# An attention and two-layer MoE kernel: v's block rows in the key buffers, key windows by DMA, and w_out's words loaded ahead of their conversion

## Chip, cores and metric

The kernel runs on one core of a Trainium2 chip. The metric is device time in microseconds (us) of one execution; three runs of a kernel are shown by their median. A profile is one more execution, with its own time.

## What is computed

Three stages follow one another. Attention works per head on 768 tokens with a window of 16 to either side, and on 24 block summaries (the maximum of the keys and the mean of the values over 32 tokens). The result goes through two feed-forward layers; the first has a softmax gate and a layer norm.

```python
k_sum = k.reshape(B, H, nb, block, D).max(axis=3)
v_sum = v.reshape(B, H, nb, block, D).mean(axis=3)
scores_all = np.concatenate([scores_l_m, scores_s], axis=-1)   # near keys (masked), block keys
a = softmax(scores_all);  attn = a @ np.concatenate([v, v_sum], axis=2)
...
h = x @ w_in;  solu = h * softmax(h)
ln = (solu - mu) / np.sqrt(var + 1e-06) * g_ln
x = ln @ w_out
...
h = x @ w_in2;  out = elu(h) @ w_out2
```

Weights come as float64, q, k and v as float32; B, H, S, D are 2, 8, 768, 64, the model width is 512, the layers 1024 and 2048 wide, and there are 1536 tokens.

## The kernel before

Attention is cut into 24 units of 64 queries, 12 for each of the two batches. Unit n has four steps: `attn_s(n)` copies the unit's 96 keys from `k_sb` into a window buffer `kw` on GpSimd (POOL), makes the scores on TensorE (PE, tile `s_ps`), adds the mask on VectorE (DVE, `sm`), takes the exponential on ScalarE (ACT) and divides on POOL; `attn_p(n)` transposes (`p_ps`, copied to `pT`); `attn_x(n)` multiplies with the value window `vw` (`x_ps`) and splits the result into a high and a low part `xT`. Every product of the two layers is three matmuls of such halves (`mm3x`). The first layer takes 128 tokens (j) at a time: products in `h`, a row maximum and two passes over 1024 columns for the norm (`ffn1_ln`), transposes to `t_ps` that ACT copies and DVE splits into `lnT` (`ffn1_tr`), and products with `w_out` in `y_ps`.

`convert` makes a float32 pair out of float64 words: a DMA of the words into a slot, an absolute value on ACT (`conv`), a clamp on POOL, three integer operations on DVE, and a copy on ACT and a difference on DVE for the two halves. The slots lie in the tiles `y0` to `y2` (shown as y_65 to y_67), two in each, which hold the first layer's result only later; the six are `early`. w_in's eight chunks use the slots in turn, w_out's eight chunks use two slots (`early[k % 2]`), and for w_out the layer norm's gain `gT` is multiplied in on POOL. The mean of v's blocks (`sum_v`, matmuls to `vs_ps`) reads six row tiles `v_rows`, which lie in y1 and y2, so in the same memory as four of the six slots.

A loop over 24 ticks sets the order of the calls. Tick t makes half of a row of the first layer (`mm_in`), the scores of unit t+6, the transposes of unit t+4 and the values of unit t+3; a dictionary `converts` says in which ticks w_out's chunks are converted. For SyncE (SP), which issues all DMAs, this order is kept as it is written. On the other engines a scheduler orders the instructions at build time, and each engine then runs them in that order. The four PSUM buffers of the tag "b" are shared by `vs_ps`, `s_ps`, `p_ps`, `x_ps`, `t_ps` and `y_ps`. A DMA gets one of eight semaphores in turn, so that a DMA is issued only when the one eight places ahead has landed.

Of the kernel before, what the change touches and what calls it, by code (L numbers as in the profile page):

```python
# [49 lines left out]
def tile_kernel(ctx: ExitStack, tc: tile.TileContext, qd, kT, v, w_in, w_out, g_ln, w_in2, w_out2,  # L50
                ident_d, mask_d, avg_d, out):
    nc = tc.nc
    scale = 1.0 / math.sqrt(D)
# [7 lines left out]

    y = [com.tile([128, KD, TC], F32, name=f"y{i}") for i in range(NTOK // TC)]
    flat = [t.rearrange("p d s -> p (d s)") for t in y]
    rows = [[t[:, i * DM:(i + 1) * DM] for i in range(KD * TC // DM)] for t in flat]
    stage = [[t.bitcast(I32)[:, i * 1024:(i + 1) * 1024].rearrange("p (k f) -> p k f", k=KD)
              for i in range(KD * TC // 1024)] for t in flat]

# [3 lines left out]
    p_k = ctx.enter_context(tc.tile_pool(name="p_k", bufs=1, side="left", reuse_waits="tile"))  # L71
    p_at = tc.alloc_tile_pool(name="p_at", bufs=2, side="left", reuse_waits="tile")
# [6 lines left out]
    w_out_hl = [chunk(p_w, "w", KF1, "w_out") for _ in range(KF1)]  # L79
    lnT_hl = [p_w.tile([128, KF1, TB], F32R, tag=f"lnT{i}", name="lnT") for i in range(2)]  # L80
    gT = p_ln.tile([128, KF1], F32, name="gT")
    negh = p_ln.tile([128, 1], F32, name="negh")
    dump = p_ln.tile([128, F1], BF16, name="dump")
    mask = p_at.tile([128, 3, KW], F32, name="mask", bufs=1)
    kws = [p_at.tile([128, NP, KW], F32, name=f"kw{i}", bufs=1) for i in range(NBUF)]
    vws = [p_at.tile([128, DM], F32, name=f"vw{i}", bufs=1) for i in range(NBUF)]
    avg = p_at.tile([128, 128 + NB], F32, name="avg", bufs=1)
    nc.gpsimd.memset(negh, -0.5)

    def copy_pool(out_, in_):  # L90
        nc.gpsimd.tensor_scalar(out_, in_, 1.0, 0.0, op0=ALU.mult, op1=ALU.add)


    def lo_of(out_, x, hi):
        nc.vector.tensor_tensor(out_, x, hi.bitcast(F32), op=ALU.subtract)  # L95
# [7 lines left out]

    def convert(bits, src, hi, lo, g=None):
        nc.sync.dma_start(bits, src if len(src.shape) == 3 else src.rearrange("p (k f) -> p k f", k=KD))
        words = bits.rearrange("p k (f two) -> p k f two", two=2)
        low, high = words[:, :, :, 0], words[:, :, :, 1]
        hi, lo = (t if len(t.shape) == 3 else t.rearrange("p (k f) -> p k f", k=KD) for t in (hi, lo))  # L110
        a = p_k.tile([128, KD, 128], I32, tag="conv", name="conv", bufs=3)
        x = a.bitcast(F32)
        nc.scalar.activation(x, high.bitcast(F32), AF.Abs)  # L113
        nc.gpsimd.tensor_scalar(x, x, F64_HUGE, F64_TINY, op0=ALU.min, op1=ALU.max)  # L114
        nc.vector.tensor_scalar(a, a, 3, 0x3FFFFFF8, op0=ALU.logical_shift_left, op1=ALU.bitwise_and)
        nc.vector.scalar_tensor_tensor(a, high, -0x40000000, a, op0=ALU.bitwise_and, op1=ALU.bitwise_or)
        nc.vector.scalar_tensor_tensor(a, low, 29, a, op0=ALU.logical_shift_right, op1=ALU.bitwise_or)
        if g is not None:
            nc.gpsimd.tensor_scalar(x, x, g, 0.0, op0=ALU.mult, op1=ALU.add)
        nc.scalar.activation(hi, x, AF.Copy)  # L120
        lo_of(lo, x, hi)

    early = stage[0] + stage[1] + stage[2]
    v_rows = rows[1] + rows[2]

    def load_w_in(n, k):
        cs = slice(n * 512, (n + 1) * 512)
# [1 line left out]
                w_in_hl[0][:, k, cs], w_in_hl[1][:, k, cs])  # L129

    def load_w_out(k):
        convert(early[k % 2], w_out[k * 128:(k + 1) * 128, :].bitcast(I32), *w_out_hl[k], gT[:, k:k + 1])


    k_sb, q_bd, xT, live, ksum, vsum = {}, {}, {}, {}, {}, {}
# [13 lines left out]

    def sum_v(b):  # L150
        pst = psb.tile([128, DM], F32, tag="b", name="vs_ps")
        for i in range(S // 128):
            vt = v_rows[i]
            nc.sync.dma_start(vt, v[b, PAD + i * 128:PAD + (i + 1) * 128, :])
            c0 = NB - i * 4
            nc.tensor.matmul(pst, lhsT=avg[:, c0:c0 + 128], rhs=vt, start=i == 0, stop=i == S // 128 - 1)
        vsum[b] = p_at.tile([128, DM], F32, tag="vsum", name="vsum", bufs=1)
        nc.scalar.activation(vsum[b][WIN:KW, :], pst[WIN:KW, :], AF.Copy)

    def load_q(n):  # L160
        q_bd[n] = p_at.tile([128, NP, 2 * TQ], F32, tag="q", name="q_bd", bufs=4)
        nc.sync.dma_start(q_bd[n], qd[n])

    def load_v(n):
        b, t = divmod(n, NT)
        nc.sync.dma_start(vws[n % NBUF][0:WIN, :], v[b, t * TQ:t * TQ + WIN, :])

    def attn_s(n):
        b, t = divmod(n, NT)
        j, half = divmod(n, 2)  # L170
        kw = kws[n % NBUF]
        if n not in q_bd:
            load_q(n)
        if t < NBUF and n:
            copy_pool(kw[:, :, WIN:KW], ksum[b])
        copy_pool(kw[:, :, 0:WIN], k_sb[b][:, :, t * TQ:t * TQ + WIN])
        sps = psb.tile([128, NP, 128], F32, tag="b", name="s_ps")
        for p in range(NP):
            nc.tensor.matmul(sps[:, p, 0:KW], lhsT=q_bd[n][:, p, :], rhs=kw[:, p, :], start=True, stop=True)  # L179
        sm = p_at.tile([128, NP, KW], F32, tag="sm", name="sm", bufs=NBUF)  # L180
        st = p_at.tile([128, 4, NP], F32, tag="st", name="st", bufs=NBUF)
        nm, ss, ri = (st[:, i, :] for i in range(3))
        mi = 1 if t == 0 else (2 if t == NT - 1 else 0)
        for p in range(NP):
            nc.vector.tensor_tensor_reduce(sm[:, p, :], sps[:, p, 0:KW], mask[:, mi, :], -scale, 3.0e38,
                                           op0=ALU.add, op1=ALU.min, accum_out=nm[:, p:p + 1])
        for p in range(NP):
            nc.scalar.activation(sm[:, p, :], sm[:, p, :], AF.Exp, bias=nm[:, p:p + 1], scale=-1.0,
                                 accum_out=ss[:, p:p + 1])
        nc.vector.tensor_scalar(ri, ss, 1e-9, None, op0=ALU.add)  # L190
        nc.vector.reciprocal(ri, ri)  # L191
        for p in range(NP):
            nc.gpsimd.tensor_scalar(sm[:, p, :], sm[:, p, :], ri[:, p:p + 1], 1.0, op0=ALU.mult, op1=ALU.mult)  # L193
        live[n] = sm
# [132 lines left out]


    conv = [lambda n=n, k=k: load_w_in(n, k) for n in range(2) for k in range(KD)]
    conv += [lambda k=k: load_w_out(k) for k in range(KF1)]  # L330

    def more(n=1):
        for _ in range(n):
            if conv:
                conv.pop(0)()
# [57 lines left out]
    for i, t in ((0, 11), (1, 17)):  # L393
        for d in range(KD):
            after[t + d].append((mm_out, i, d))
    converts = {3: 2, 4: 1, 6: 1, 9: 2, 10: 2}
    NU = B * NT
    for t, (j, n) in enumerate(ticks):
        s_n, p_n, x_n = t + LEAD, t + LEAD - 2, t + LEAD - 3
        if t == 0:  # L400
            sum_v(1)
        elif t == 1:
            load_k(1)
        elif t == 3:
            sum_k(1)
        if x_n < NU and t:
            load_v(x_n)
        if s_n < NU:
            for u in (s_n + 1, s_n):
                if u < NU and u not in q_bd:  # L410
                    load_q(u)
            attn_s(s_n)
        mm_in(j, n)
        if p_n < NU:
            attn_p(p_n)
        for f, *args in after[t]:
            f(*args)
        if x_n < NU:
            attn_x(x_n)
        more(converts.get(t, 0))  # L420
        if t in (13, 15, 17, 18, 19, 20, 21, 22):
            load_w3()
        if x_n == NU - 1:
            p_at.release()
            p_w3 = ctx.enter_context(tc.tile_pool(name="p_w3", bufs=1, side="left", reuse_waits="tile"))
            lnT_last = [p_w3.tile([128, KF1, TB], F32R, tag=f"lnT{c}", name="lnT") for c in range(2)]
# [35 lines left out]
             f == 0, f == KF2 - 1)  # L462

    def store(i, ops, t):
        o = rows[0][t]
        r0 = i * TC + t * 128
        if i == NTOK // TC - 1 and t == NTT - 1:
            for c in range(2):
                cs = slice(c * 256, (c + 1) * 256)
                if c:  # L470
                    nc.vector.tensor_copy(o[:, cs], ops[t][:, cs])
                else:
                    nc.scalar.activation(o[:, cs], ops[t][:, cs], AF.Copy)
# [84 lines left out]
```

## Time and profile before

| | us |
|---|---|
| median of 3 runs (lowest to highest) | 510.34 (509.59 to 511.14) |
| the profiled execution, its own time | 507.9 |
| span of the profile | 505.8 |
| TensorE busy | 483.2 |
| VectorE, ScalarE, GpSimd busy | 283.5, 261.8, 131.0 |
| mean granted TensorE clock, as a share of 2.4 GHz | 0.993 |

Busy time is the time in which an engine ran at least one instruction. What the profiled execution's own time has over its span lies before and after the program's instructions.

### The profile page before, as it was taken

To read this page: it belongs to the slowest core of one execution; us is meant where nothing else is said; L and a number is where in the kernel's file an instruction comes from. 1 tells how busy PE (TensorE), PEld (TensorE's weight loads), DVE (VectorE), ACT (ScalarE), POOL (GpSimd) and SP (SyncE) were. 2 spreads that over 40 slices of the span, in tenths; PEclk is the share of its full clock that TensorE was granted. 3 is DMA by queue.
4 is the path that set the end of the run, shared out by engine and by line. 5 is a ranking of instruction groups with operands and counts; after the bars stand their busy time and mean duration, and the time that the engine had idled before them with its cause. 6 is when DMAs were issued, how large, how long until landed. Compare 5 with 4: busy or idle time off the path is not lost.

```text
span 505.8 us, 7269 instructions
## 1 busy us (share of the span) xinstructions
PE 483.2 (96%) x2616; PEld 400.5 (79%) x2616; DVE 283.5 (56%) x680; ACT 261.8 (52%) x592; POOL 131.0 (26%) x216
## 2 busy tenths in 40 slices
PE   1789997999999999999999999999999999999997
PEld 1466876888988888999888888888888888888885
DVE  3689799798458747797999622351222235122222
ACT  1675896776568436655767433352323335232333
POOL 1867688688413321322232100000000000000000
PEclk9999998999999999999999999999999999999999
DMA  8989473171313400565454000020000002000002
GB/s 302 286 296 311 132 231 120 38 233 39 115 59 116 141 1 0 208 172 166 155 173 126 1 0 0 1 84 1 1 1 0 0 1 84 1 0 0 1 0 83
DMA packets 24563, 46.53 MB, mean 92 GB/s; under 512 B 2256, under 2 KB 11088, under 8 KB 24528
## 3 DMA queue, kind: packets, MB, share of 16 engines
q1 hardware_dynamic: 24528, 46.08, 28.6%
q8 instruction: 20, 0.33, 0.3%
q14 instruction: 15, 0.12, 0.1%
HBM read 42.93 MB, written 3.15 MB: 91 GB/s over the span
## 4 chain that ended last, share of the span: by engine, by line
PE 88%; DMA 3%; DVE 3%; ACT 2%; POOL 1%; issue 1%; SPq 1%; ACTq 0%; POOLq 0%
PE h L98 13%; PE h L100 13%; PE h L99 13%; PE o_ps L98 9%; PE o_ps L99 9%; PE o_ps L100 9%; PE y_ps L98 5%; PE y_ps L100 4%; PE s_ps L179 4%; PE y_ps L99 4%; PE x_ps L215 2%; DMA q_bd<-in_qd 2%; PE p_ps L198 2%; PE t_ps L254 1%; DMA k_sb<-in_kT 1%
## 5 line engine op out<-in xcount | busy, mean ns | idle before, releaser
L454 DVE SCALAR_TENSOR_TENSOR m<-m,h 128x512 f32<-128x512 f32 x48 | 32.9, 685 | 120.0 <-ACT m L453 119.8
L452 ACT ACTIVATE m<-h 128x512 f32<-128x512 f32 x48 | 28.7, 598 | 107.5 <-PE h L100 107.2
L99 PE MATMUL h<-y_hl,w 128*128 128x512 f32 x192 | 75.9, 395 | 0.0
L100 PE MATMUL h<-y_hl,w 128*128 128x512 f32 x192 | 75.9, 395 | 0.0
L98 PE MATMUL o_ps<-w,g_hl 128*128 128x512 f32 x192 | 75.5, 393 | 0.0
L99 PE MATMUL o_ps<-w,g_hl 128*128 128x512 f32 x192 | 75.4, 393 | 0.0
L98 PE MATMUL h<-y_hl,w 128*128 128x512 f32 x192 | 75.2, 395 | 0.0
L100 PE MATMUL o_ps<-w,g_hl 128*128 128x512 f32 x192 | 66.9, 392 | 0.0
L114 POOL TENSOR_SCALAR conv<-conv 128x512 f32<-128x512 f32 x48 | 36.4, 761 | 67.2 <-ACT conv L113 65.9
L193 POOL TENSOR_SCALAR sm<-sm,st 128x120 f32<-128x120 f32 x96 | 44.9, 484 | 16.7 <-DVE st L191 15.8
L95 DVE TENSOR_TENSOR g_hl<-m,g_hl 128x512 fp32r<-128x512 f32 x48 | 33.9, 707 | 24.4 <-ACT g_hl L455 24.4
L455 ACT ACTIVATE g_hl<-m 128x512 fp32r<-128x512 f32 x48 | 30.3, 630 | 32.5 <-DVE m L454 32.5
L179 PE MATMUL s_ps<-kw,q_bd 128*128 128x120 f32 x192 | 29.6, 301 | 15.9 <-DMA q_bd<-in_qd 13.3
L98 PE MATMUL y_ps<-lnT,w_out 128*128 128x384 f32 x128 | 44.0, 344 | 0.3 <-DVE lnT L95 0.2
L100 PE MATMUL y_ps<-lnT,w_out 128*128 128x384 f32 x128 | 43.1, 338 | 0.0
L99 PE MATMUL y_ps<-lnT,w_out 128*128 128x384 f32 x128 | 43.1, 336 | 0.0
L99 PEld LDWEIGHTS h<-y_hl,w 128*128 128x128 f32 x192 | 36.1, 188 | 8.6
L98 PEld LDWEIGHTS o_ps<-w,g_hl 128*128 128x128 f32 x192 | 36.1, 188 | 8.5
L100 PEld LDWEIGHTS h<-y_hl,w 128*128 128x128 f32 x192 | 36.1, 188 | 8.5
L98 PEld LDWEIGHTS h<-y_hl,w 128*128 128x128 f32 x192 | 36.1, 188 | 8.5
L100 PEld LDWEIGHTS o_ps<-w,g_hl 128*128 128x128 f32 x192 | 36.1, 188 | 8.2
L99 PEld LDWEIGHTS o_ps<-w,g_hl 128*128 128x128 f32 x192 | 36.1, 188 | 8.2
(77 smaller groups left out, 913.1 us busy)
## 6 DMA issues: line engine op xcount, KB each, us to landing
y<-in_w_in SPq DMA_DIRECT2D x20, 512.0 KB, 4.6
y<-in_w_out SPq DMA_DIRECT2D x16, 512.0 KB, 4.3
q_bd<-in_qd SPq DMA_DIRECT2D x24, 256.0 KB, 5.0
vw<-in_v SPq DMA_DIRECT2D x24, 192.0 KB, 4.2
bits<-in_w_out SPq DMA_DIRECT2D x8, 512.0 KB, 3.5
k_sb<-in_kT SPq DMA_DIRECT2D x8, 400.0 KB, 5.5
y<-in_v SPq DMA_DIRECT2D x12, 256.0 KB, 5.4
out<-y SPq DMA_DIRECT2D x11, 256.0 KB, 2.3
```

The lines of the kernel that those rows point to most:

```text
L95: nc.vector.tensor_tensor(out_, x, hi.bitcast(F32), op=ALU.subtract)
L98: nc.tensor.matmul(ps, lhsT=l[0][ls], rhs=r[0][rs], start=first, stop=False)
L99: nc.tensor.matmul(ps, lhsT=l[0][ls], rhs=r[1][rs], start=False, stop=False)
L100: nc.tensor.matmul(ps, lhsT=l[1][ls], rhs=r[0][rs], start=False, stop=last)
L114: nc.gpsimd.tensor_scalar(x, x, F64_HUGE, F64_TINY, op0=ALU.min, op1=ALU.max)
L179: nc.tensor.matmul(sps[:, p, 0:KW], lhsT=q_bd[n][:, p, :], rhs=kw[:, p, :], start=True, stop=True)
L193: nc.gpsimd.tensor_scalar(sm[:, p, :], sm[:, p, :], ri[:, p:p + 1], 1.0, op0=ALU.mult, op1=ALU.mult)
L198: nc.tensor.transpose(pps[:KW, p, :], live[n][:, p, :], ident)
L215: nc.tensor.matmul(xps[ds, p, :], lhsT=vw[:KW, p * 128 + hh * D:p * 128 + (hh + 1) * D], rhs=pT[:KW, p, hh * TQ:(hh + 1) * TQ], start=True ...
L452: nc.scalar.activation(m, h2, AF.Relu, scale=-1.0)
L454: nc.vector.scalar_tensor_tensor(m, m, -1.0, h2, op0=ALU.add, op1=ALU.max)
L455: nc.scalar.activation(gh, m, AF.Copy)
```

## The change

1. `sum_v` loads v's rows into a tile `v_sb` of the pool that holds `k_sb` (tag "k", two buffers) and no longer into y1 and y2. The two buffers serve k of batch 0, v of batch 0, v of batch 1 and k of batch 1, the last three one after the other in the same memory.
2. There are four `kw` buffers in place of three. From unit 12 on (batch 1) a DMA fills the key window (`load_kw`), one tick ahead; POOL copies it for units 0 to 11 only.
3. w_out's words go into all six slots (`early[k % 6]`), and their DMAs stand apart from the conversions: `fetches` issues them in ticks 2 to 9, `converts` makes the conversions in ticks 4 to 10. The first ACT instruction of each such conversion keeps its place in the order of the calls (`pin`).
4. The gain is multiplied in by ACT's copy (`scale=g`) and by DVE's difference; POOL's multiplication is gone.
5. One of the second layer's early conversions (`load_w3` in tick 17 or 18) moves behind the ticks: there are seven in place of eight, in other ticks.

```diff
-    rows = [[t[:, i * DM:(i + 1) * DM] for i in range(KD * TC // DM)] for t in flat]
+    rows = [t[:, i * DM:(i + 1) * DM] for t in flat[:1] for i in range(KD)]
...
+    def load_words(bits, src):
         nc.sync.dma_start(bits, src if len(src.shape) == 3 else src.rearrange("p (k f) -> p k f", k=KD))
...
-        nc.scalar.activation(x, high.bitcast(F32), AF.Abs)
+        first = nc.scalar.activation(x, high.bitcast(F32), AF.Abs)
+        if pin:
+            tc.keep_in_program_order(first)
...
-        if g is not None:
-            nc.gpsimd.tensor_scalar(x, x, g, 0.0, op0=ALU.mult, op1=ALU.add)
-        nc.scalar.activation(hi, x, AF.Copy)
-        lo_of(lo, x, hi)
+        if g is None:
+            nc.scalar.activation(hi, x, AF.Copy)
+            lo_of(lo, x, hi)
+        else:
+            nc.scalar.activation(hi, x, AF.Copy, scale=g)
+            nc.vector.scalar_tensor_tensor(lo, x, g, hi.bitcast(F32), op0=ALU.mult, op1=ALU.subtract)
...
     def load_w_out(k):
-        convert(early[k % 2], w_out[k * 128:(k + 1) * 128, :].bitcast(I32), *w_out_hl[k], gT[:, k:k + 1])
+        load_words(early[k % 6], w_out[k * 128:(k + 1) * 128, :].bitcast(I32))
+
+    def convert_w_out(k):
+        convert(early[k % 6], None, *w_out_hl[k], gT[:, k:k + 1], pin=True)
...
+        v_sb = p_k.tile([128, NP, S + 2 * PAD], F32, tag="k", name="v_sb", bufs=2).rearrange("p a s -> p (a s)")
         for i in range(S // 128):
-            vt = v_rows[i]
+            vt = v_sb[:, i * DM:(i + 1) * DM]
...
+    def load_kw(n):
+        b, t = divmod(n, NT)
+        if NCOPY <= n < B * NT:
+            nc.sync.dma_start(kws[n % NKW][:, :, 0:WIN],
+                              kT[b, :, :, t * TQ:t * TQ + WIN].rearrange("p d s -> d p s"))
...
-        copy_pool(kw[:, :, 0:WIN], k_sb[b][:, :, t * TQ:t * TQ + WIN])
+        if n < NCOPY:
+            copy_pool(kw[:, :, 0:WIN], k_sb[b][:, :, t * TQ:t * TQ + WIN])
...
-    converts = {3: 2, 4: 1, 6: 1, 9: 2, 10: 2}
+    converts = {4: 1, 5: 1, 6: 1, 7: 1, 8: 1, 9: 1, 10: 2}
+    fetches = {2: 1, 3: 1, 4: 1, 5: 1, 6: 1, 7: 1, 8: 1, 9: 1}
...
+            load_kw(s_n + 1)
             attn_s(s_n)
...
-        more(converts.get(t, 0))
-        if t in (13, 15, 17, 18, 19, 20, 21, 22):
+        for _ in range(fetches.get(t, 0)):
+            words.pop(0)()
+        for _ in range(converts.get(t, 0)):
+            parts.pop(0)()
+        if t in (13, 15, 19, 20, 21, 22, 23):
             load_w3()
```

The order of the instructions shows at three places. The first is SP near the start, where v's rows of batch 0 are loaded and behind them two chunks of w_in's words and the queries of unit 2 (`q_bd`); first before:

```order
L154 DMA y_66<-in_v 128x512 x4
L154 DMA y_67<-in_v 128x512 x2
L107 DMA y_66<-in_w_in 128x1024 x2
L162 DMA q_bd<-in_qd 128x512
L166 DMA vw_103<-in_v 96x512
L374 DMA gT<-in_g_ln 128x8
```

The same place with the change:

```order
L168 DMA v_sb<-in_v 128x512 x6
L109 DMA y_66<-in_w_in 128x1024 x2
L176 DMA q_bd<-in_qd 128x512
L180 DMA vw_104<-in_v 96x512
L396 DMA gT<-in_g_ln 128x8
```

Nothing changes its place there, but the two chunks of words no longer go into memory that v's rows occupy.

The second place is PE in tick 6, where the first rows of the first layer are transposed (`t_ps`); before, between the products of one row and the scores of unit 13:

```order
L100 MATMUL h<-w_in_83,xT 128x512
L198 MATMUL p_ps<-ident,sm 120x128
L254 MATMUL t_ps<-ident,ln 128x128 x2
L198 MATMUL p_ps<-ident,sm 120x128
L254 MATMUL t_ps<-ident,ln 128x128
L198 MATMUL p_ps<-ident,sm 120x128 x2
L254 MATMUL t_ps<-ident,ln 128x128 x13
L215 MATMUL x_ps<-pT,vw_102 64x64 x8
L179 MATMUL s_ps<-kw_100,q_bd 128x120 x4
```

The same place with the change, from the last four transposes on (ahead of them stand the unit's `p_ps` x4, `t_ps` x4, three products, `t_ps` x8 and nine products):

```order
L101 MATMUL h<-w_in_84,xT 128x512
L102 MATMUL h<-w_in_83,xT 128x512
L275 MATMUL t_ps<-ident,ln 128x128 x4
L236 MATMUL x_ps<-pT,vw_103 64x64 x8
L200 MATMUL s_ps<-kw_100,q_bd 128x120 x4
```

Sixteen transposes in one piece have become pieces of 4, 8 and 4, with 3 and 9 products of `h` between them.

The third place is DVE at the same point of the program, where the low halves of `lnT` are made; before:

```order
L234 TENSOR_REDUCE st<-h 128x1
L115 TENSOR_SCALAR conv<-conv 128x512
L95 TENSOR_TENSOR lnT<-t_ps,lnT 128x4x128
L116 SCALAR_TENSOR_TENSOR conv<-y_65,conv 128x512
L237 SCALAR_TENSOR_TENSOR ln,st<-h,ln 128x1024
L239 TENSOR_SCALAR st<-st 128x1
L117 SCALAR_TENSOR_TENSOR conv<-y_65,conv 128x512
L95 TENSOR_TENSOR lnT<-t_ps,lnT 128x4x128
```

The same place with the change:

```order
L125 SCALAR_TENSOR_TENSOR conv<-y_65,conv 128x512
L262 SCALAR_TENSOR_TENSOR st<-st 128x1
L126 SCALAR_TENSOR_TENSOR conv<-y_65,conv 128x512
L97 TENSOR_TENSOR lnT<-t_ps,lnT 128x4x128 x3
L264 SCALAR_TENSOR_TENSOR st<-st 128x1
L255 TENSOR_REDUCE st<-h 128x1
```

A conversion's two operations and a pass over a row of `h` stood between the first and the second `lnT`; now three stand together, and the row maximum comes behind them. From the program's start to the second `lnT`, DVE has two L115, two L116, two L117, one difference for w_out, one L234 and one L237 fewer than before (counted in the whole order).

## Rows read from the trace of the kernel before

**Rows 1.** Page, part 1: busy time of each engine.
```profile
PE 483.2 (96%) x2616; PEld 400.5 (79%) x2616; DVE 283.5 (56%) x680; ACT 261.8 (52%) x592; POOL 131.0 (26%) x216
```

**Rows 2.** Waits of PE: line, what it waited for, us in total, times, longest.
```profile
PE s_ps L179 <- DMA q_bd<-in_qd: 13.3, 2, 10.9
```

**Rows 3.** Stretches: length, busy us (PE, PEld, DVE, ACT, POOL), clock, DMA, GB/s.
```profile
10.00:15.00 5.00, 4.11 (x18) 3.67 (x19) 1.52 (x15) 2.40 (x10) 1.63 (x3) 1.00 1.04 393
15.00:20.00 5.00, 5.00 (x16) 2.28 (x14) 4.80 (x15) 2.59 (x10) 4.38 (x7) 1.00 0.79 238
...
25.00:30.00 5.00, 4.79 (x49) 3.89 (x47) 2.81 (x20) 3.09 (x14) 1.83 (x4) 0.74 1.03 380
60.00:85.00 25.00, 22.29 (x172) 18.07 (x171) 23.97 (x82) 21.57 (x64) 19.65 (x35) 1.00 0.46 134
85.00:100.00 15.00, 14.88 (x119) 12.44 (x119) 11.23 (x38) 10.03 (x32) 9.29 (x15) 0.89 0.30 103
100.00:120.00 20.00, 20.00 (x138) 16.99 (x135) 18.31 (x63) 15.31 (x45) 16.36 (x28) 1.00 0.52 158
300.00:350.00 50.00, 50.00 (x218) 40.49 (x217) 15.71 (x22) 19.31 (x31) 0.00 (x0) 1.00 0.06 22
```

**Rows 4.** Chain that ended last, 14 to 30 us: start, us, what.
```profile
14.36 3.69 PE vs_ps L156 x8
...
18.43 5.69 DMA q_bd<-in_qd
...
24.26 2.03 PE s_ps L179 x8
...
27.97 1.10 PE s_ps L179 x8
```

**Rows 5.** Timeline of SP: start, us, DMAs issued.
```profile
8.91 3.47 SPq L154 DMA_DIRECT2D y<-in_v  x6
16.35 2.04 SPq L107 DMA_DIRECT2D y<-in_w_in  x2
```

**Rows 6.** Timeline of POOL, 22 to 25 us.
```profile
22.63 2.56 POOL L91 TENSOR_SCALAR vw<-vsum 24x512 f32<-24x512 f32 x3
```

**Rows 7.** Timeline of PE, 20 to 22 and 81 to 87 us; in brackets the idle time ahead.
```profile
20.47 1.34 PE L198 MATMUL p_ps<-ident,sm 128*120 128x128 f32 x4 [0.28 <-POOL sm L193]
...
81.77 0.69 PE L215 MATMUL x_ps<-pT,vw 120*64 120x64 f32 x16 [0.29 <-DVE lnT L95]
84.87 1.43 PE L179 MATMUL s_ps<-kw,q_bd 128*128 128x120 f32 x8 [2.42 <-DVE lnT L95]
```

**Rows 8.** Timeline of DVE, 79 to 86 us.
```profile
79.14 1.23 DVE L234 TENSOR_REDUCE st<-h 128x1 f32<-128x1024 f32 x1 [0.65 <-PE h L100]
80.28 0.42 DVE L115 TENSOR_SCALAR conv<-conv 128x512 int32<-128x512 int32 x1
...
81.63 0.68 DVE L116 SCALAR_TENSOR_TENSOR conv<-y,conv 128x512 int32<-128x512 int32 x1
82.23 1.22 DVE L237 SCALAR_TENSOR_TENSOR ln<-h,ln 128x1024 f32<-128x1024 f32 x1
...
83.44 0.78 DVE L117 SCALAR_TENSOR_TENSOR conv<-y,conv 128x512 int32<-128x512 int32 x1
84.14 0.68 DVE L95 TENSOR_TENSOR lnT<-t_ps,lnT 128x512 fp32r<-128x512 f32 x1
84.74 0.87 DVE L95 TENSOR_TENSOR w_out<-conv,w_out 128x512 fp32r<-128x512 f32 x1
```

**Rows 9.** Groups of instructions: line, operation, count | busy us, mean ns | idle ahead.
```profile
L91 POOL TENSOR_SCALAR kw<-k_sb 128x384 f32<-128x384 f32 x24 | 13.7, 573 | 20.8 <-PE s_ps L179 12.9 <-DMA k_sb<-in_kT 7.1 <-PE p_ps L198 0.5
L119 POOL TENSOR_SCALAR conv<-conv,gT 128x512 f32<-128x512 f32 x8 | 5.5, 693 | 2.0 <-DVE conv L117 2.0
L116 DVE SCALAR_TENSOR_TENSOR conv<-y,conv 128x512 int32<-128x512 int32 x36 | 26.7, 742 | 0.3
```

**Rows 10.** DMAs issued in 12.0 to 12.4 us: count, KB each, us to landing.
```profile
y<-in_v SPq DMA_DIRECT2D x1, 256.0 KB, 5.5
```

More of the change, by code (lines that the diff above doesn't have):

```diff
@@ L37 @@
 NBUF = 3
+NKW = 4
+NCOPY = 12
 NG = 6
@@ L84, in tile_kernel @@
     mask = p_at.tile([128, 3, KW], F32, name="mask", bufs=1)
-    kws = [p_at.tile([128, NP, KW], F32, name=f"kw{i}", bufs=1) for i in range(NBUF)]
+    kws = [p_at.tile([128, NP, KW], F32, name=f"kw{i}", bufs=1) for i in range(NKW)]
     vws = [p_at.tile([128, DM], F32, name=f"vw{i}", bufs=1) for i in range(NBUF)]
@@ L100, in mm3x, with convert @@
         nc.tensor.matmul(ps, lhsT=l[1][ls], rhs=r[0][rs], start=False, stop=last)
-    def convert(bits, src, hi, lo, g=None):
+    def load_words(bits, src):
         nc.sync.dma_start(bits, src if len(src.shape) == 3 else src.rearrange("p (k f) -> p k f", k=KD))
+    def convert(bits, src, hi, lo, g=None, pin=False):
+        if src is not None:
+            load_words(bits, src)
         words = bits.rearrange("p k (f two) -> p k f two", two=2)
@@ L117, in convert @@
         nc.vector.scalar_tensor_tensor(a, low, 29, a, op0=ALU.logical_shift_right, op1=ALU.bitwise_or)
-        if g is not None:
-            nc.gpsimd.tensor_scalar(x, x, g, 0.0, op0=ALU.mult, op1=ALU.add)
-        nc.scalar.activation(hi, x, AF.Copy)
-        lo_of(lo, x, hi)
+        if g is None:
[4 more added lines that the diff above has]
+            nc.vector.scalar_tensor_tensor(lo, x, g, hi.bitcast(F32), op0=ALU.mult, op1=ALU.subtract)
     early = stage[0] + stage[1] + stage[2]
-    v_rows = rows[1] + rows[2]
     def load_w_in(n, k):
@@ L170, in attn_s @@
         j, half = divmod(n, 2)
-        kw = kws[n % NBUF]
+        kw = kws[n % NKW]
         if n not in q_bd:
             load_q(n)
-        if t < NBUF and n:
+        if t < NKW and n:
             copy_pool(kw[:, :, WIN:KW], ksum[b])
-        copy_pool(kw[:, :, 0:WIN], k_sb[b][:, :, t * TQ:t * TQ + WIN])
+        if n < NCOPY:
+            copy_pool(kw[:, :, 0:WIN], k_sb[b][:, :, t * TQ:t * TQ + WIN])
         sps = psb.tile([128, NP, 128], F32, tag="b", name="s_ps")
@@ L329, in tile_kernel @@
     conv = [lambda n=n, k=k: load_w_in(n, k) for n in range(2) for k in range(KD)]
-    conv += [lambda k=k: load_w_out(k) for k in range(KF1)]
+    words = [lambda k=k: load_w_out(k) for k in range(KF1)]
+    parts = [lambda k=k: convert_w_out(k) for k in range(KF1)]
     def more(n=1):
@@ L464, in store @@
     def store(i, ops, t):
-        o = rows[0][t]
+        o = rows[t]
         r0 = i * TC + t * 128
```

## The prediction

> **What bounds the kernel now.** I read the busy times first: PE is busy in 483.2 of 505.8 us, no other engine in more than 56% [rows 1]. Only PE's 22.6 idle us, and time in which it runs slower than it could, are there to be won. In the second layer there is none: from 300 to 350 us PE is busy in all of 50.00 at full clock, DVE in 15.71 [rows 3], and the change leaves that code alone. So I looked at PE's waits and then at the chain around each.
>
> The largest is the start: the first scores wait 10.9 us for queries, and 2 such waits make 13.3 [rows 2]. The loads ahead of that first wait are the same before and after the change. The other wait for queries, 13.3 - 10.9 = 2.4 us, ends at 24.26, and the chain tells its cause: PE multiplies v's rows from 14.36 to 18.05, this releases an issue on SP, the queries of unit 2 are issued at 18.43, land 5.69 us later, and PE starts [rows 4]. SP had last issued before that with v's rows, 8.91 to 12.38, and came to the next words of w_in only at 16.35 [rows 5]: these words go into memory that v's rows occupied. While SP stood, the DMA engines ran dry: 393 GB/s in 10 to 15 us, 238 in 15 to 20 [rows 3].
>
> The last large hole lies at 81 to 85 us: after 16 transposes the values of unit 9 wait 0.29 and the scores of unit 13 wait 2.42 us for a subtraction on DVE that frees a PSUM buffer [rows 7]. DVE was not idle then. In its row stood a conversion's operations and a pass over a row of h: 81.63, 82.23, 83.44, and only at 84.14 the subtraction [rows 8]. From 60 to 85 us DVE is busy in 23.97 of 25.00 [rows 3]; there it sets the pace.
>
> Both holes cost a second time. The granted clock is 0.74 in 25 to 30 us, and 0.89 in 85 to 100, which at two levels (1.2 and 2.4 GHz) is 15 x 0.11 = 1.65 us of lost work [rows 3]; in each case PE had just stood for more than 2.3 us.
>
> **The start.** v's rows now have memory of their own, so w_in's two chunks wait only for the DMA eight places ahead to land, and SP goes on where it stopped, at 12.38. From there on what counts is the bytes under way: the last of v's rows is issued at about 12.05 (the last 0.33 of the piece that ends at 12.38) and lands 5.5 us later, at 17.5 [rows 5, 10]; behind them 2 x 524 KB at 393 GB/s take 2.67 us and the queries' 262 KB 0.67, so these land at 20.8, in place of 18.43 + 5.69 = 24.1. PE ends its transposes at 20.47 + 1.34 = 21.8 [rows 7] and goes on at once. The scores take 1.1 us at full clock [rows 4], to 22.9. Then comes a new wait: the values of units 0 and 1 need POOL's copies of the block means, three from 22.63 to 25.19, so 0.85 each [rows 6]; the first is done at 23.5, the second at 24.3. With 0.6 us for each unit's values (81.77: 0.69 in which the last overlaps the next [rows 7]) the scores of unit 3 start at 25.0, against 27.97. Gain 2.97, taken as **3.0 us**. Bounds: without POOL's wait 24.3, a gain of 3.7; if the clock still falls through the shorter waits, about 1.3 less (24.26: 2.03 against 1.10, and the values a third longer), 1.7.
>
> Whether it lasts depends on DVE, full from 60 to 85 us: the gain reaches that stretch only if DVE's work, which w_in's words feed, moves forward as well. The words land earlier by as much as the queries do, so I let it last.
>
> **The hole at 81.** Transposes now come as 4, 8 and 4 with 3 and 9 products between, and three subtractions stand together on DVE. Nine products alone give PE 9 x 0.23 = 2.1 us in which the buffers come free. Ahead of the second subtraction DVE has less to do: two L115 (0.42), two L116 (0.68), two L117 (0.78), one L95 (0.87), one L234 (1.23) and one L237 (1.22) fewer, together 7.1 us [rows 8]. So DVE should be early there by more than the 2.71 us that PE waited. I leave 0.3 us as a wait and take **2.4 us**, and the clock's 1.65, **1.7 us**. Bounds: 0 and 2.7 for the wait, 0 and 1.7 for the clock.
>
> **Given back on DVE.** The 7.1 us are moved, not gone: all eight conversions must be done before the first y_ps is complete. From 85 to 100 us DVE idles 15.00 - 11.23 = 3.77 us, from 100 to 120 another 1.69 [rows 3]. These take 5.5; the rest, 7.1 - 5.5 = 1.6, delays y_ps: **-1.6 us**. Bounds: 0, if the products that the new order puts between y_ps cover it, and -7.1 if the idle time can't be used.
>
> **Costed at nothing.** POOL's multiplications (8 x 0.69) and 12 of its 24 copies (0.57 each) go [rows 9]; POOL was not what ended a wait of PE there, except for units 2 and 3. DVE's difference keeps its size, 128x512. The 12 new DMAs of 197 KB each (262 KB land in 5.5 us even in a full queue [rows 10]) stand right behind the queries of the same unit, and after 24.26 no scores waited for queries [rows 2]; DMA share is 0.46, 0.30 and 0.52 there [rows 3]. If that cover went, each lateness would count once per unit. w_out's words no longer hold up SP's queue until a conversion is done. The conversion that moves behind the ticks costs DVE about 2.7 us between 210 and 300; PE's first need of its product comes seven tiles later, so nothing.
>
> **POOL's share of DVE's time.** L116 reads two SBUF operands and takes 0.742 us on average [rows 9], 0.68 at 81.63 [rows 8]; over the 36 this is 2.2 us if POOL is the cause. Of POOL's work some 12.4 of the page's 131.0 us go, so between 0 and 2.2; I put 0 into the sum and half, 1.1, into its upper bound. The Trainium skill (SBUF — State Buffer, section "Who interferes with whom") says that DVE with two SBUF inputs and a GpSimd operation that reads SBUF exclude each other for the whole instruction. By it the 12.4 us of POOL work that go could free as much of DVE; the trace agrees with it in direction, with 0.742 against 0.68 us.
>
> **Sum.** 3.0 + 2.4 + 1.7 - 1.6 = 5.5 us, on the profiled execution 507.9 - 5.5 = 502.4. Its 507.9 is 2.4 under the median of the runs, 510.34, so the median becomes **504.8**. The forecast's own range is from 3.7 + 2.7 + 1.7 + 0 + 1.1 = 9.2 (501.1) to 3.6 us of gain (506.7).
>
> **Rivals.**
> - *One hole only* (gain 1.5 to 3.6, at 3.0: 507.3). The hole at 81 stays in another form: four PSUM buffers are shared by 16 transposes, values and scores as before, and DVE still has a row maximum and a conversion behind the third subtraction. For it: DVE is 96% busy there. Against it: the 7.1 us.
> - *DVE takes it all* (within 0.3%, at 510). k of batch 1 must now wait until v's products of batch 1 are done on PE, and DVE's maxima of those keys stand in its row. If they come 3 us late, the start's gain is gone, and with the -7.1 bound so is the second. Against it: the new order puts these maxima behind the last conversion of w_in.
> - *Slower: late key windows.* From unit 12 on the scores need a DMA in rows of 384 bytes. It decides if 12 windows come late by more than 5.5 / 12 = 0.46 us each; at 0.9 us each the time is 504.8 + 10.8 = 515.6. For it: each is behind queries and values in one queue. Against it: DMA share and the missing waits named above.
>   Twice the 0.5 us that 197 KB take at 393 GB/s [rows 3] would add 0.5 us per window, if nothing hid it: 12 x 0.5 = 6.0, so 510.8.
>   The Trainium skill (DMA: Bandwidth & Descriptors, section "Specifications") asks for 512 bytes and more for line rate and names a read-modify-write below; no row here shows it.
>
> **Chances.** Forecast 0.56; more than its range 0.06; one hole only 0.16; within 0.3% 0.12; slower 0.10. A run of this kernel can't tell less than 0.3% (1.5 us) from no change. Faster is 0.56 + 0.06 + 0.16 = 0.78. The range 501.1 to 509.3 leaves out the slower case, the upper half of the unchanged one and a tail below: 0.10 + 0.06 + 0.03.
>
> **What would show it.** Right: the scores of unit 2 start near 21.8 us with no wait for queries, unit 3's near 25.0; no wait over 1 us of PE for lnT around 76 to 82; clock 1.00 in both stretches; DVE over 90% busy from 85 to 115. Wrong: PE waits for kw DMAs after 70 us, for y_ps's w_out, or the DVE maxima of k idle for their DMA at 43 to 47.

## The result, and the profile after

The change makes the kernel faster: median 502.58 us of four runs (502.39 to 502.74) against 510.4 of four runs of before (509.59 to 511.14), ratio 0.984, 95% interval 0.983 to 0.986. The profiled executions are 5.5 us apart (507.9 and 502.39), just the forecast sum. The medians are 7.8 apart, 2.3 more than forecast.

The busy times [rows 1] changed little; GpSimd lost 11.9 us, VectorE has 3.7 more:

```profile
PE 480.0 (96%) x2616; PEld 397.4 (79%) x2616; DVE 287.2 (57%) x680; ACT 262.8 (53%) x592; POOL 119.1 (24%) x198
```

TensorE's waits after (columns as in [rows 2]): the queries are waited for once, at the start; new are the wait of the values for POOL's block means (`vw`) and, at 46.84 us, one of the scores for ACT's copy of batch 1's block means (`vsum`).

```profile
PE s_ps L200 <- DMA q_bd<-in_qd: 11.3, 1, 11.3
PE p_ps L219 <- POOL sm L214: 1.3, 3, 0.5
PE s_ps L200 <- ACT vsum L172: 0.9, 1, 0.9
...
PE x_ps L236 <- POOL vw L93: 0.7, 2, 0.4
```

The stretches of [rows 3], after:

```profile
15.00:20.00 5.00, 5.00 (x13) 2.17 (x12) 4.79 (x18) 3.68 (x13) 4.48 (x6) 1.00 1.04 398
25.00:30.00 5.00, 3.92 (x31) 2.67 (x31) 4.67 (x23) 5.00 (x21) 3.78 (x6) 1.00 1.04 367
...
60.00:85.00 25.00, 24.93 (x195) 20.74 (x194) 20.57 (x82) 21.85 (x69) 15.24 (x31) 1.00 0.81 245
85.00:100.00 15.00, 15.00 (x126) 11.88 (x126) 13.68 (x54) 13.81 (x44) 10.89 (x19) 1.00 0.51 151
100.00:120.00 20.00, 20.00 (x149) 17.78 (x148) 15.44 (x48) 12.56 (x33) 11.92 (x19) 1.00 0.33 93
```

The transfers no longer run dry in 15 to 20 us (398 GB/s, before 238), the clock is 1.00 throughout, and TensorE is busy in 24.93 and 15.00 us where it was busy in 22.29 and 14.88. VectorE idles 4.4 us in 60 to 85, where it had idled 1.0.

TensorE's timeline, at the two places of [rows 7] (the scores of units 2, 3, 10 and 13):

```profile
22.60 0.33 PE L219 MATMUL p_ps<-ident,sm 128*120 128x128 f32 x1 [0.45 <-POOL sm L214]
22.76 1.06 PE L200 MATMUL s_ps<-kw,q_bd 128*128 128x120 f32 x8
24.23 0.69 PE L236 MATMUL x_ps<-pT,vw 120*64 120x64 f32 x16 [0.41 <-POOL vw L93]
25.25 0.69 PE L236 MATMUL x_ps<-pT,vw 120*64 120x64 f32 x16 [0.33 <-POOL vw L93]
25.86 1.15 PE L200 MATMUL s_ps<-kw,q_bd 128*128 128x120 f32 x8
...
60.70 1.15 PE L200 MATMUL s_ps<-kw,q_bd 128*128 128x120 f32 x8
...
79.29 0.60 PE L275 MATMUL t_ps<-ident,ln 128*128 128x128 f32 x4
80.43 1.15 PE L200 MATMUL s_ps<-kw,q_bd 128*128 128x120 f32 x8
```

And VectorE's timeline at the place of [rows 8], where the subtraction that frees PSUM no longer waits behind other work:

```profile
77.97 1.87 DVE L97 TENSOR_TENSOR lnT<-t_ps,lnT 128x512 fp32r<-128x512 f32 x3
79.76 0.14 DVE L264 SCALAR_TENSOR_TENSOR st<-st 128x1 f32<-128x1 f32 x1
79.83 1.21 DVE L255 TENSOR_REDUCE st<-h 128x1 f32<-128x1024 f32 x1
```

### The profile page after: what moved, and what is told of

The parts are those of the page before. It is cut to its first block, busy times and chain, and to the rows that moved or that the text cites. A ratio compares the mean times of both kernels' runs of the same rounds, so it can differ in the third digit from the quotient of the medians.

```text
span 500.5 us, 7260 instructions
## 1 busy us (share of the span) xinstructions
PE 480.0 (96%) x2616; PEld 397.4 (79%) x2616; DVE 287.2 (57%) x680; ACT 262.8 (53%) x592; POOL 119.1 (24%) x198
## 4 chain that ended last, share of the span: by engine, by line
PE 85%; DVE 5%; DMA 3%; ACT 2%; POOL 2%; issue 1%; SPq 1%; POOLq 0%; ACTq 0%
PE h L100 13%; PE h L102 13%; PE h L101 13%; PE o_ps L100 9%; PE o_ps L101 9%; PE o_ps L102 9%; PE s_ps L200 4%; PE y_ps L101 3%; PE y_ps L102 3%; PE y_ps L100 3%; PE x_ps L236 3%; PE p_ps L219 2%; DMA bits<-in_w_out 1%; PE t_ps L275 1%; DMA q_bd<-in_qd 1%
## 5 line engine op out<-in xcount | busy, mean ns | idle before, releaser
L101 PE MATMUL y_ps<-lnT,w_out 128*128 128x384 f32 x128 | 43.0, 338 | 0.3 <-DVE lnT L97 0.3
L100 PE MATMUL y_ps<-lnT,w_out 128*128 128x384 f32 x128 | 43.1, 339 | 0.0
L102 PE MATMUL y_ps<-lnT,w_out 128*128 128x384 f32 x128 | 42.8, 337 | 0.0
L100 PE MATMUL h<-w_in,xT 128*128 128x512 f32 x96 | 40.5, 422 | 0.8 <-ACT xT L239 0.8
```

The lines of the kernel that those rows point to most:

```text
L100: nc.tensor.matmul(ps, lhsT=l[0][ls], rhs=r[0][rs], start=first, stop=False)
L101: nc.tensor.matmul(ps, lhsT=l[0][ls], rhs=r[1][rs], start=False, stop=False)
L102: nc.tensor.matmul(ps, lhsT=l[1][ls], rhs=r[0][rs], start=False, stop=last)
```

## The experiments

Two questions stood open: why the median fell 2.3 us more than the profiled execution, and what each part is worth. The kernel before is shown by its median beside each group on the same chip: 510.41 (first four), 509.44 (next four), 510.0 (last four). The changed kernel itself ran again beside the last four alone (e8); a cost below is the difference to its first median, 502.58, and for the middle four, on whose chip the kernel before was 1 us faster, it is uncertain by about as much.

The last column shows where in the profiled execution the time lies: the start of the first scores; the time from there to the 297th matmul, in all kernels but e9 the first of unit 10's scores; and the time from that to the 1201st, the first transpose of row 6 (rows counted from 0, as the units). The second and third do not contain the first transfers.

| run | median us (lowest to highest) | ratio to before, 95% | first scores; to unit 10; to row 6 |
|---|---|---|---|
| before (the prediction's profile) | 510.4 (509.59 to 511.14) | | 10.86; 50.73; 129.11 |
| changed (first result) | 502.58 (502.39 to 502.74) | 0.984, 0.983 to 0.986 | 11.27; 49.43; 124.13 |
| e0_before | 509.95 (508.46 to 512.6) | 0.9997, 0.998 to 1.002 | 11.61; 52.28; 128.96 |
| e1_v_memory_alone | 509.01 (507.6 to 511.27) | 0.9975, 0.996 to 0.9995 | 10.90; 49.84; 130.94 |
| e2_v_rows_back | 506.58 (506.15 to 506.96) | 0.993, 0.990 to 0.995 | 11.69; 52.94; 124.88 |
| e3_pool_copies_all | 504.46 (503.34 to 505.04) | 0.988, 0.986 to 0.991 | 11.44; 49.42; 125.31 |
| e4_converts_as_before | 506.51 (505.65 to 507.58) | 0.994, 0.9925 to 0.996 | 12.09; 49.43; 128.06 |
| e5_gain_on_pool | 504.63 (503.54 to 504.88) | 0.990, 0.989 to 0.992 | 12.02; 49.43; 125.39 |
| e6_w3_ticks_as_before | 503.05 (502.81 to 503.62) | 0.988, 0.986 to 0.989 | 11.99; 49.16; 124.72 |
| e7_v_in_w_out_memory | 504.88 (503.56 to 507.55) | 0.992, 0.989 to 0.996 | 11.70; 50.69; 124.31 |
| e8_after_again | 502.34 (501.69 to 502.66) | 0.985, 0.983 to 0.987 | 11.67; 49.42; 124.16 |
| e9_keys_early_maxima_pinned | 502.95 (502.8 to 503.36) | 0.987, 0.985 to 0.988 | 11.76; 49.39; 124.51 |
| e10_keys_early_maxima_late | 502.52 (501.88 to 503.48) | 0.986, 0.984 to 0.9875 | 12.86; 48.68; 124.67 |
| e11_pool_work_all_back | 504.0 (503.01 to 504.8) | 0.9885, 0.987 to 0.990 | 11.08; 49.42; 125.40 |

**e0_before**: no edit.

> The kernel before, unchanged, five times more: its profiled execution took 507.9 us, 2.4 less than its median of 510.4, where the changed kernel's profiled execution (502.39) and median (502.58) agree. Theory: the two holes of TensorE (2.4 us at 24, 2.4 us at 85) cost granted clock by an amount that differs from one execution to the next; then executions of 510 us show a mean clock below 0.993 (2.4 of 506 us are 0.5%, so near 0.988), and one of 508 us shows 0.993. Rival: the executions differ in when transfers land; then spans differ by 2 us at the same clock of 0.993.

Twelve executions lay between 508.46 and 512.6 us. Those with clock 0.993 had spans from 506.7 to 509.8, the one with 0.989 had 510.8, the one with 0.996 had 508.1, the three with 0.997 had 507.0 to 508.0. Both theories hold in part: the lowest clock goes with the longest span, but most of the scatter stands at one clock. The profile of this run shows what differed in one of them, in TensorE's timeline:

```profile
26.53 1.12 PE L179 MATMUL s_ps<-kw,q_bd 128*128 128x120 f32 x8 [3.70 <-DMA q_bd<-in_qd]
29.49 0.78 PE L179 MATMUL s_ps<-kw,q_bd 128*128 128x120 f32 x2
...
63.90 0.82 PE L179 MATMUL s_ps<-kw,q_bd 128*128 128x120 f32 x5
...
87.19 1.15 PE L179 MATMUL s_ps<-kw,q_bd 128*128 128x120 f32 x8 [2.42 <-DVE lnT L95]
```

The same program waited 3.70 us for the queries of unit 2, where the prediction's profile showed 2.4, and its unit 3 started at 29.49 and not at 27.97. The hole at 85 us is the same to the hundredth. The profile on which the prediction rested (span 505.8) caught a short wait, and early first transfers too (first scores at 10.86, here at 11.61); of the 51 executions of before that followed none had a span under 506.0.

**e1_v_memory_alone**, the kernel before with:

```diff
+        v_sb = p_k.tile([128, NP, S + 2 * PAD], F32, tag="k", name="v_sb", bufs=2).rearrange("p a s -> p (a s)")
-            vt = v_rows[i]
+            vt = v_sb[:, i * DM:(i + 1) * DM]
```

> The kernel before with part 1 alone: v's rows in memory of their own (the key buffers). Theory (SyncE stood because w_in's words went into memory that v's rows occupied): the wait of 2.4 us for queries at 24 us is gone, the scores of unit 3 start near 26 us in place of 28, the hole of 2.4 us at 85 us stays, and the time falls by 0.9 to 2.5 us, to 508 to 509.5. Rival (VectorE takes it all, because k of batch 1 now waits for v's products): same start, but the scores of unit 10 no earlier than at 61.6 us, and 510.4. Rival (the stall is of another cause): the wait at 24 us stays.

The cause of the stall is shown: no second wait for queries, unit 3 starts at 25.50, unit 10 at 60.74, so the first rival misses place and time. The time fell by 1.4 us only, within the theory's range. Where the rest went: the way to unit 10 is 2.4 us shorter than in e0, and the way from there to row 6 is 2.0 longer (table). The hole at 85 us stays as several waits of 0.2 to 0.9 us from 80 to 86 and a longer one behind, 1.8 us for lnT; TensorE idles 2.93 and 2.66 us in these two stretches (before: 2.71 and 0.12 [rows 3]).

```profile
60.00:85.00 25.00, 22.07 (x174) 17.80 (x168) 22.37 (x77) 20.18 (x64) 21.98 (x40) 1.00 0.49 150
85.00:100.00 15.00, 12.34 (x109) 10.23 (x110) 12.66 (x40) 12.07 (x33) 9.73 (x15) 1.00 0.34 112
```

**e2_v_rows_back**, the changed kernel with `vt = v_rows[i]` and `v_rows` in y1 and y2 again.

> The changed kernel with part 1 undone: v's rows in y1 and y2 again, everything else as changed. Theory: TensorE waits again about 2.4 us for queries at 24 us, with a granted clock below 1.0 in 25 to 30 us, and 2 us or more of it last to the end: 504.5 to 506. Rival (VectorE swallows the start in any case, since only 0.9 us of the gain were left at 61 us): 503 to 503.6.

It costs 4.0 us (506.58 against 502.58), 0.6 more than the theory's range allows; its cause is right and the rival falls. In the profiled executions 3.5 us lie ahead of unit 10 and last; 0.75 come from there to row 6, where a wait of 1.2 us for lnT is new. The wait for queries is back, longer than in the prediction's profile, and the clock in 25 to 30 us is 0.68:

```profile
26.75 2.01 PE L200 MATMUL s_ps<-kw,q_bd 128*128 128x120 f32 x8 [3.85 <-DMA q_bd<-in_qd]
```

**e4_converts_as_before**, the changed kernel with:

```diff
-    converts = {4: 1, 5: 1, 6: 1, 7: 1, 8: 1, 9: 1, 10: 2}
+    converts = {3: 2, 4: 1, 6: 1, 9: 2, 10: 2}
```

> The changed kernel with the conversions of w_out's words in the ticks of before (two in tick 3, one in 4, one in 6, two in 9, two in 10); words still loaded apart and v's rows in their own memory. TensorE's row keeps the first 16 transposes in pieces with products between; on VectorE a row maximum and a conversion's operation stand again between the first four subtractions for lnT. Theory (the 7.1 us that left VectorE's row close the hole at 85): a wait of TensorE for lnT of 1 us or more comes back between 76 and 88 us, 503.6 to 505.6. Rival (pieces of transposes are enough): no such wait and 502.1 to 503.1.

It costs 3.9 us, more than the theory's range, all of it between unit 10 and row 6 (128.06 us against 124.13), and not as one wait for lnT: TensorE is busy in 23.57 of 25.00 us in 60 to 85 and in 14.00 of 15.00 in 85 to 100. VectorE's row (timeline) has the row maximum and a conversion's operation between the subtractions again:

```profile
79.76 0.68 DVE L97 TENSOR_TENSOR lnT<-t_ps,lnT 128x512 fp32r<-128x512 f32 x1
80.36 1.21 DVE L255 TENSOR_REDUCE st<-h 128x1 f32<-128x1024 f32 x1
81.49 0.67 DVE L97 TENSOR_TENSOR lnT<-t_ps,lnT 128x512 fp32r<-128x512 f32 x1
82.09 0.41 DVE L124 TENSOR_SCALAR conv<-conv 128x512 int32<-128x512 int32 x1
82.42 0.68 DVE L97 TENSOR_TENSOR lnT<-t_ps,lnT 128x512 fp32r<-128x512 f32 x1
...
84.28 0.15 DVE L264 SCALAR_TENSOR_TENSOR st<-st 128x1 f32<-128x1 f32 x1
84.35 0.41 DVE L97 TENSOR_TENSOR xT<-x_ps,xT 128x256 fp32r<-128x256 f32 x1
```

Late by it are the last step of the norm of the third row, row 2 (L264, 84.28; in the changed kernel 79.76) and xT (84.35), for which TensorE waited 0.95 us:

```profile
84.82 0.50 PE L102 MATMUL h<-w_in,xT 128*128 128x512 f32 x1 [0.95 <-DVE xT L97]
```

The third row's transposes start at 90.04 us in place of 82.56 (the first scores 0.8 later), and behind them 0.88 us are waited for lnT, at 93.66 and not in the window that the theory named. From 62 to 195 us TensorE idles 2.68 us in place of 0.33; the other 1.6 us of the 3.9 are not idle time, and what they are stays open. The rival falls: the first two rows' transposes stood in pieces of 4, 8 and 4 here too. Whether VectorE's order would be enough with sixteen transposes in one piece was not tried.

**e3_pool_copies_all** (`NCOPY = 24`), **e5_gain_on_pool** (the gain in `nc.gpsimd.tensor_scalar(x, x, g, ...)` again) and **e11_pool_work_all_back** (both), on the changed kernel.

> The changed kernel with the key windows of all 24 units copied by GpSimd (no window DMAs). If GpSimd's relief was worth nothing, as costed: 502.1 to 503.1, the VectorE operation L125 at the same mean length. If GpSimd slows VectorE instruction by instruction: 12 copies of 0.57 us come back, and the time rises by up to 6.8 us, to between 504 and 509. If the window DMAs cost something: faster than 502.1.

> The changed kernel with the gain multiplied in on GpSimd again, 8 operations of 0.69 us, as before. Costed at nothing: 502.1 to 503.1. If GpSimd's row is what made the 12 key copies cost 1.9 us (504.46 against 502.58, for 6.8 us of work), these 5.5 us cost about 1.5 us: 504.1.

> The changed kernel with all of GpSimd's work of before: the 24 key copies and the gain. Each alone gave 504.5 and 504.6. If what they cost is GpSimd's own time in the stretch from 80 to 130 us, they add: 506 to 507. If each only used up the same slack or shuffled the order: 504 to 505.

Costed at nothing, GpSimd's relief was worth 1.4 to 2.0 us (504.46, 504.63, 504.0), and the two parts don't add. That VectorE runs freer does not account for it: the group of L125 (L116 before, [rows 9], 742 ns) with GpSimd busy in 134.5 us (e11), in 127.4 (e5) and in 119.1 (changed):

```profile
L125 DVE SCALAR_TENSOR_TENSOR conv<-y,conv 128x512 int32<-128x512 int32 x36 | 27.1, 752 | 0.3
```

```profile
L125 DVE SCALAR_TENSOR_TENSOR conv<-y,conv 128x512 int32<-128x512 int32 x36 | 26.6, 739 | 0.2
```

```profile
L125 DVE SCALAR_TENSOR_TENSOR conv<-y,conv 128x512 int32<-128x512 int32 x36 | 26.7, 743 | 0.3
```

The mean is 9 ns longer in e11 (0.3 us over the 36), and 4 shorter in e5, which cost the most. Single operations do get longer beside GpSimd's; in the trace of before:

```profile
15.53 0.62 POOL L114 TENSOR_SCALAR conv<-conv 128x512 f32<-128x512 f32 x1 [0.52 <-ACT conv L113]
16.25 5.18 POOL L193 TENSOR_SCALAR sm<-sm,st 128x120 f32<-128x120 f32 x8
```

```profile
15.72 0.98 DVE L116 SCALAR_TENSOR_TENSOR conv<-y,conv 128x512 int32<-128x512 int32 x1
18.77 0.68 DVE L116 SCALAR_TENSOR_TENSOR conv<-y,conv 128x512 int32<-128x512 int32 x1
```

Of the 36, 16 ran with no GpSimd operation beside them and took 0.67 to 0.70 us; the 20 others took 0.67 to 1.10. The Trainium skill (SBUF — State Buffer, section "Who interferes with whom") lets such an operation, with two SBUF inputs, contend with a GpSimd operation that reads SBUF. The trace agrees for some operations, and not for the one at 18.77, which lies wholly beside GpSimd's division.

What the three runs have in common is 1.2 to 1.3 us more between unit 10 and row 6, and nothing more ahead of it, and a wait that the changed kernel has not: the third row's transposes for VectorE's lnT, 0.98 us in e5, 0.95 in e11 and 0.38 in e3. In e5:

```profile
84.19 1.06 PE L275 MATMUL t_ps<-ident,ln 128*128 128x128 f32 x8 [0.98 <-DVE lnT L97]
```

Of waits over 0.3 us only this one is new; that the rest came through the order that the scheduler makes of each build is likely and not shown.

**e6_w3_ticks_as_before**, the changed kernel with `if t in (13, 15, 17, 18, 19, 20, 21, 22)`.

> The changed kernel with eight early conversions for the second layer in the ticks of before (17 and 18 among them) in place of seven. Costed at nothing: 502.1 to 503.1. If VectorE has no room there: one conversion more, about 2.7 us, delays lnT of the second group and shows as waits of y_ps between 140 and 200 us, up to 505.3.

503.05, as costed; no wait of y_ps, and one new wait of 0.5 us for lnT. The 0.5 us over the changed kernel are less than the spread of the first transfers (its first scores started at 11.99 us, the changed kernel's at 11.27).

**e7_v_in_w_out_memory**, the changed kernel with v's rows in buffers of w_out's tag, whose tiles are allocated when a chunk is converted:

```diff
-        v_sb = p_k.tile([128, NP, S + 2 * PAD], F32, tag="k", name="v_sb", bufs=2).rearrange("p a s -> p (a s)")
+        v_sb = [p_w.tile([128, 2, DM], F32, tag="w", bufs=KF1, name="v_sb") for _ in range(3)]
```

> The changed kernel with v's rows in the memory that w_out's halves take later, so that k of batch 1 no longer waits for the products with v's rows of batch 1 (the issue waits 5.1 us on SyncE, to 42.4 us). Theory: that wait gives back what the changed kernel loses against the kernel with v's rows in y1 and y2 in 40 to 50 us (TensorE's lost time 2.93 against 1.23 us): 501 to 502. Rival (VectorE's work in 60 to 100 us swallows it): 502.4 to 502.8. Rival (the earlier keys push w_in's words back in the queue): slower than 503.

Slower, by none of the three as stated: the third rival's time came true, but w_in's last words landed 6.8 us after their issue, in the changed kernel 6.7. The keys of batch 1 landed 7 us earlier (38.9 to 43.3 us against 45.8 to 50.2). They no longer wait for v's products, and the scheduler put their maxima (ksum) ahead of the last operations on w_in's last chunk on VectorE:

```profile
42.56 0.92 DVE L158 TENSOR_REDUCE ksum<-k_sb 128x24 f32<-128x768 f32 x1
43.40 0.75 DVE L97 TENSOR_TENSOR w_in<-conv,w_in 128x512 fp32r<-128x512 f32 x1
44.41 0.94 DVE L158 TENSOR_REDUCE ksum<-k_sb 128x24 f32<-128x768 f32 x1
45.92 1.80 DVE L158 TENSOR_REDUCE ksum<-k_sb 128x24 f32<-128x768 f32 x2
49.05 0.68 DVE L97 TENSOR_TENSOR w_in<-conv,w_in 128x512 fp32r<-128x512 f32 x1
```

TensorE waited 1.85 us for w_in at 49 us, and the way to unit 10 was 1.3 us longer than in the changed kernel. Hence the next two.

**e9_keys_early_maxima_pinned** and **e10_keys_early_maxima_late**, e7 with the maxima of batch 1 kept in the order of the calls (`tc.keep_in_program_order`), called in tick 1 and in tick 3; e8 is the changed kernel beside them.

> The changed kernel, unchanged, beside the others on one chip. Its four executions had lain within 502.39 to 502.74, with the first scores at 11.27 us; in the runs since then the first scores started between 10.9 and 12.1 us, whatever the kernel. If that start (when the first keys and queries land) is all that varies: 502.4 to 503.5, clock 1.0 in every execution, against 508 to 512 for the kernel before.

> The kernel of the run with v's rows in w_out's memory, and the block maxima of k of batch 1 kept in the order of the calls on VectorE, behind w_in's last chunk (there two of the four stood ahead of that chunk's operations, and TensorE waited 1.9 us for it). Theory (that place was the cause of the loss): no wait for w_in at 49 us, and the time is 501.5 to 502.5, under the changed kernel on the same chip by 0.5 to 1.5. Rival (VectorE's work in 60 to 100 us sets the pace whatever happens ahead): equal to the changed kernel within 0.3%.

> As the last, with the maxima two ticks later in the order of the calls, behind the first two rows' passes over h. On TensorE's row 8 transposes stand in one piece right ahead of the values of unit 9 and the scores of unit 13, where the changed kernel has 4. Theory (pieces and VectorE's order both count): a wait for lnT of 0.5 us or more near 80 us, and slower than the last run by 0.5 us or more. Rival: equal to it.

e8 came out at 502.34, a little under its range; its executions again lie within 1 us. The wait of 1.85 us for w_in is gone in e9 and e10, and their time is that of the changed kernel within 0.2%, as both rivals say. The reason that e9's rival gives, VectorE's work behind it, is not shown: the way to unit 10 was no shorter in e9 than in the changed kernel (49.39 us against 49.43), though the keys landed from 40.4 us on in place of 45.8, so there was no gain to swallow. In e10 it was 0.75 shorter, of which 0.5 were lost by row 6, with a wait of 0.51 us for xT. There 8 transposes stood in one piece ahead of the values, with no wait for lnT, so a piece of 8 costs nothing at this place. No version here beats the changed kernel.

## Why the prediction was right, and where its sum was not

**The start: right in cause, too small.** Forecast 3.0 (27.97 to 25.0), the scores of unit 3 started at 25.86, of which 0.41 is the first transfer landing later (11.27 against 10.86). The new wait for POOL's copies is there, 0.41 and 0.33 us, and one not forecast, 0.45 for POOL's division, which with the late transfer put unit 2 at 22.76 and not 21.8. Against the profile of before that leaves 2.1 us, and at unit 10 only 0.9 (61.59 to 60.70): in 40 to 50 us TensorE idles 1.60 us, where before it idled none, 0.88 of it in the wait for ACT's copy `vsum`, which stood behind w_in's last chunk. No term of the sum held this wait. Against e0's profile it is 3.6 and 3.2, and undoing the part costs 4.0. The mis-sized term is the wait removed: 2.4 us in the one execution read, 3.70 in the next. The steps' bound of 3.7 came from that one execution too, and the range's lower gain of 3.6 us is not worked out from any of the bounds.

**It lasts only with the other part.** "I let it last" depended, as written, on VectorE's work moving forward. Alone the part gave 1.4 us; everything else without it gave 510.41 - 506.58 = 3.8. 1.4 + 3.8 = 5.2 of the 7.8; the rest, 2.6 us (uncertain by about 1, the width of e1's interval to either side), exists only when both are there.

**The hole at 81: right.** No wait of TensorE for lnT is left up to 195 us. From 62 to 195 us TensorE's busy time was 129.92 of 133.00 in the profile of before, 128.61 in e0's, and 132.67 after (sums of a table of windows):

```profile
sum 133.00, PE 129.92 PEld 112.12 DVE 97.57 ACT 88.84 POOL 69.25; mean PE 21.65 PEld 18.69 DVE 16.26 ACT 14.81 POOL 11.54
```

```profile
sum 133.00, PE 128.61 PEld 110.85 DVE 97.88 ACT 88.92 POOL 71.99; mean PE 21.43 PEld 18.47 DVE 16.31 ACT 14.82 POOL 12.00
```

```profile
sum 133.00, PE 132.67 PEld 114.92 DVE 99.58 ACT 91.47 POOL 58.39; mean PE 22.11 PEld 19.15 DVE 16.60 ACT 15.24 POOL 9.73
```

That is 3.08 idle us plus the clock's 1.7, less 0.33: 4.45 against the first, and 4.39 - 0.33 = 4.06 against e0's, whose clock stayed full behind the same hole. Forecast 2.4 + 1.7 = 4.1. e4 shows that the pieces of transposes alone do not give it, and that the moved conversions, so VectorE's order, are needed.

**Given back on VectorE: wrong.** Of the 1.6 us almost nothing shows: those 0.33 idle us are all of TensorE's from 62 to 195, no y_ps wait falls there, and the one behind, at 213.00, is of 0.30 us. The step took VectorE for full up to 120 us. In 85 to 100 it did take up 2.45 of the 3.77 idle us, but in 100 to 120 it was busy in 15.44 of 20.00, less than before (18.31); the sign "over 90% busy from 85 to 115" failed narrowly (26.43 of 30.00, 88%). The moved work found room, the end of the bound that said 0.

**Costed at nothing:** right for the window DMAs (no wait for kw; they landed a median 4.4 us after issue) and the conversion that moved (e6); for w_out's words no wait shows, but no run undid that part alone; wrong for GpSimd's work, 1.4 to 2.0 us. The 0.68 us at 81.63 that the prediction set against the mean of 0.742 does not stand for an idle GpSimd, which was busy beside it all the time (80.42 to 82.46); the 16 operations without GpSimd beside them, 0.67 to 0.70 us, bear the same comparison out.

**The rivals.** "DVE takes it all" is nearly what the first part does alone (e1, 1.4 us). Late key windows: no wait for kw anywhere. VectorE's maxima of batch 1's keys waited for no DMA either. One hole only: no.

**The sum.** On the profiled execution 5.5 us came out by errors that cancel. 1200 matmuls lie ahead of the first transpose of row 6 in both kernels; before, in TensorE's timeline:

```profile
61.59 1.15 PE L179 MATMUL s_ps<-kw,q_bd 128*128 128x120 f32 x8
190.70 0.82 PE L254 MATMUL t_ps<-ident,ln 128*128 128x128 f32 x6
```

and after:

```profile
184.83 0.38 PE L275 MATMUL t_ps<-ident,ln 128*128 128x128 f32 x2
```

Up to unit 10 the gain is 0.9 (forecast 3.0), from there to row 6 (190.70 - 184.83) - 0.9 = 5.0 (forecast 2.4 + 1.7 - 1.6 = 2.5; 4.45 of them in the idle time and clock above), and behind it 0.6 is lost, half of it in the wait at 213.00: spans 505.8 - 500.5 = 5.3. That the sum met the profiled execution's 5.5 is luck. Carried to the median with a constant 2.4 us, it fell short, because more than half of these 2.4 us, as far as one more execution shows, were made by the wait that the change removes: in e0, unit 10 came 2.3 us later than in the prediction's profile, 0.75 of it by the first transfers, the rest on the way to unit 10, where the wait for queries was 1.25 longer. With the wait gone, the eight executions of the changed kernel lie within 501.69 to 502.74 us.

## What to carry to other kernels

A wait for a transfer varies from one execution to the next, so what its removal is worth is read from several executions; where the profiled execution is faster than the median of the runs, ask which wait was short in it. When a later stretch is paced by another engine, an early gain and that engine's relief are one gain: the two parts alone were worth 5.2 us here, together 7.8. Before a transfer is moved up, ask what ends the waits behind it: in e9 the keys came 5 us earlier and the way to unit 10 was no shorter, with the wait of 0.87 us for `vsum` still there. A build-time scheduler answers an earlier transfer by moving its consumer up; look at what that now stands ahead of.

## What was not expected of the hardware

The granted clock did not answer in the same way to the same hole. Behind TensorE's wait of 2.42 us for lnT it was 0.66 in 85 to 90 us in one execution of before, and 1.00 in another (e0):

```profile
85.00:90.00 5.00, 5.00 (x22) 4.26 (x23) 4.01 (x17) 2.92 (x13) 3.09 (x5) 0.66 0.61 218
```

```profile
85.00:90.00 5.00, 2.40 (x15) 1.89 (x16) 5.00 (x17) 3.95 (x9) 2.67 (x5) 1.00 0.78 269
90.00:95.00 5.00, 5.00 (x24) 4.05 (x24) 1.58 (x10) 2.62 (x10) 4.54 (x8) 1.00 0.09 36
```

And the first scores, which wait for the first transfers (in e7 for GpSimd's copy of the first keys), started between 10.86 and 12.86 us over these 14 profiles, whatever the kernel: a difference of 0.5 us between two single executions tells nothing here.
